# Delta rule and maxout FFN on one core: inverse squares of the key norms from one root, first diagonal blocks copied from PSUM, first solution turned in halves, weight conversions behind x

## The chip, the cores and the metric

The kernel runs on one core of a Trainium2 chip. The metric is the device time of one execution in microseconds (us), as the median of three runs. Engines are named as in the profile: PE is TensorE, DVE is VectorE, ACT is ScalarE, POOL is GpSimd, SP is SyncE, which here only issues transfers.

## The reference

Two parts follow each other. The first is a delta rule over 768 tokens for 4 batches and 8 heads of 48 dimensions; the second is a maxout FFN over 3072 tokens, with three weights 384 to 768 and one 768 to 384. All arrays are fp32.

```python
# q, k, v: [4, 8, 768, 48]   beta: [4, 8, 768]
k_n = k / (np.linalg.norm(k, axis=-1, keepdims=True) + 1e-06)
state = np.zeros((B, H, D, D), dtype=np.float32)
for t in range(S):
    kt, vt, bt = (k_n[:, :, t], v[:, :, t], beta[:, :, t, None])
    y[:, :, t] = np.einsum('bhd,bhde->bhe', q[:, :, t], state)
    v_old = np.einsum('bhde,bhd->bhe', state, kt)
    state = state + bt[:, :, :, None] * np.einsum('bhd,bhe->bhde', kt, vt - v_old)
x = y.transpose(0, 2, 1, 3).reshape(4 * 768, 384)
h = np.maximum(np.maximum(x @ w1, x @ w2), x @ w3)
out = h @ w_out
```

## The kernel before

**Tiling.** The 768 tokens of a sequence are cut into 12 chunks of 64, taken for 2 batches at a time on the 128 partitions. Two chunks for all four batches make a group of 512 rows of x, so there are 6 groups, m = 0 to 5. A chunk's recurrence needs the inverse of a triangular 64x64 matrix for each head and batch. It is made from two 32x32 diagonal blocks, inverted on DVE, and an off-diagonal part made by matmuls on PE.

**The solver.** `solve(m)` inverts the diagonal blocks of group m. It first takes the diagonal of the blocks, which holds the squared norms of the keys (`ksum`), and makes two things of it in `bl` (128x32): the norm plus 1e-6, and beta divided by its square. The root is taken on ACT (L261), and a refinement of it and all that follows on DVE (L262 to L266, then L519 to L525). `norms_of(m, bl)` turns the norms on DVE into the layout of the values (four transpositions, L281, into `nrm`); `scale` multiplies the values by them on POOL (L287). The blocks are multiplied by the factors (L538), and then come the steps, each of them one product (L552) and one difference (L556) on DVE with few columns at first. The generator yields after each step; `some(solving, n)` issues n of them between other work.

**The order of work.** There is no scheduler. Each engine executes what the Python code issued, in that order, and waits on semaphores for what it needs. `ffn(m)` is a generator over the FFN of group m; at each of its yields `i` a table (`LINKS`, `FIRST` for group 0, `EARLY_LINKS`) says which pieces of the recurrence of the next group are issued. A table entry is a letter and a number: k is `old_k` (p_k on PE, then `v_t` minus `p_k` on DVE, L743), q `old_q`, u `new` (p_u on PE from that `v_t`, L759), y `to_y`, s `step`, x `to_x`, P a Gram matrix with its mask, M a mask alone, N `load_blocks` for the group after next. In the steady table the entries around the change are

```python
5: "g2 g3 p1", 6: "u0 N0", 7: "V1 N1", 8: "s0 y0 N2", 9: "x0", 10: "k1 q1",
11: "u1 w0", 13: "y1 x1 s1", 14: "X0 w1", 16: "P0", 17: "X1 K0 K1 K2 K3",
```

`solve(m + 2)` and its head (all up to the first yield) are issued at i = 8 behind "s0 y0 N2", and its first steps at i = 9. `load_blocks` of N0, N1 and N2 issues 16 transfers each from POOL's queue (L364), with a memset ahead of each eight. It acts only while a group m + 2 exists, so in the FFNs of groups 1 to 3; the solves of groups 3, 4 and 5 start in the FFNs of groups 1, 2 and 3.

**Weights.** The FFN's weights go through a conversion: `weights()` fetches the fp32 bits in pieces of 128 columns and splits each into two halves. ACT does three scalings (L238 to L240), DVE one shift (L250) and POOL one addition (L254). `some(conv, 1)` issues one piece; the POOL addition of a piece is issued when the next piece is.

**The opening.** Before the first FFN, `keys(n)` makes the Gram matrix p_g of a unit in PSUM, ACT or DVE copies it to `at` (L423), and `to_blocks` copies four 32x32 block groups of `at` out of SBUF (L465, L467) into a tile in `wo_sb`. `first_blocks` transposes that tile on DVE (L471). Group 0 is then solved with blocks of size 32 in rows of 16, its solution is transposed as a whole (L564), copied into `ut` by `placed` (L496), and `ut` is transposed again by `halves_t` into `t` (L633, L635). Then follow `halves_z`, `halves_u`, `turn_t1`, `join_z`, `join_u` (the off-diagonal part, p_e, p_f, p_z, p_j), `old_k`, `old_q`, `new`, `to_y`, `to_x`, and the head of `solve(1)`; then the FFN of group 0 begins with p_h (L1161) and its maximum on DVE (L1175).

Of the kernel before, what the change touches and what calls it, by code (L numbers as in the profile page):

```python
# [14 lines left out]
ALU = mybir.AluOpType  # L15

C = 64
DP = 64
BL = 32
HB = 16  # L20
# [3 lines left out]
def kernel(  # L24
# [196 lines left out]
    def weights():  # L221

        waiting = None
        for dst, _, (a, b) in pieces:
            bits = staged.popleft().rearrange("p (a b two) -> p a b two", a=a, two=2)
            low, high = bits[:, :, :, 0], bits[:, :, :, 1]
            mant = work.tile([128, 384], U32, name="mant", bufs=2)
            up = work.tile([128, 384], I32, name="up", bufs=2)  # L230
            mant_v = mant.rearrange("p (a b) -> p a b", a=a)
            up_v = up.rearrange("p (a b) -> p a b", a=a)
            halves = [
                up.bitcast(t)[:, i::2].rearrange("p (a b) -> p a b", a=a)
                for i, t in enumerate((I16, FP16))
            ]

            nc.scalar.mul(mant_v.bitcast(FP32), high.bitcast(FP32), 2.0**-112)  # L238
            nc.scalar.mul(halves[0], low, 2.0**-29)
            nc.scalar.mul(halves[1], high.bitcast(FP32), 2.0**-64)  # L240
            if waiting:
                joined(*waiting)
            waiting = dst, mant, mant_v, up_v
            yield
        joined(*waiting)
        yield

    def joined(dst, mant, mant_v, up_v):
# [9 lines left out]

    def norm(out, ksum, root, t):

        nc.scalar.sqrt(root, ksum)  # L261
        nc.vector.tensor_scalar_max(t, root, 1e-30)  # L262
        nc.vector.reciprocal(t, t)
        nc.vector.tensor_tensor(out=t, in0=t, in1=ksum, op=ALU.mult)
        nc.vector.tensor_tensor(out=t, in0=t, in1=root, op=ALU.add)
        nc.vector.tensor_scalar(  # L266
            out=out, in0=t, scalar1=0.5, scalar2=1e-6, op0=ALU.mult, op1=ALU.add
        )

    def small(name, *shape):  # L270
# [27 lines left out]
    nrm_0 = const.tile([128, 2, 2, H], FP32, name="nrm_0")  # L298
    bl_0 = []

    def first_norms():
        nc.vector.transpose(out=nrm_0.rearrange("p c g h -> p (c g h)"), in_=bl_0[0])

# [150 lines left out]

    def to_blocks(n, engines):


        cc, g = divmod(n, 2)
        for i, engine in enumerate(engines):
            bb, half = divmod(i, 2)  # L460
            r, x0 = block(bb, half), 16 * cc + 8 * g
            to = in_rows(in_wo(0))[r, x0 : x0 + H]
            of = ats[n][r, :, BL * half : BL * (half + 1)]
            if engine is nc.scalar:
                engine.copy(to, of)  # L465
            else:
                engine.tensor_copy(to, of)  # L467

# [19 lines left out]

    def placed(cc, i, copy=nc.vector.tensor_copy, xs_of=slice(0, 2 * H)):
        bb, half = divmod(i, 2)  # L490
        r = block(bb, half)
        to = ut[cc][r, :, :, BL * half : BL * (half + 1)].rearrange(
            "p g h i -> p (g h) i"
        )
        of = in_rows(xs[0])[r, :, 16 * cc : 16 * (cc + 1)].rearrange("p i x -> p x i")
        copy(to[:, xs_of], of[:, xs_of])  # L496

    def solve(m):
# [11 lines left out]
        elif m > 2:  # L510
            nc.scalar.copy(y, zero.to_broadcast(y.shape))
        bl = small("bl", BL)
        norm(bl, diagonal(x), small("root_bl", BL), small("nt_bl", BL))
        if m == 1:
            y = ps_two("y_p").rearrange("p b (j i) -> p (b j) i", i=BL)
            nc.scalar.copy(y, zero.to_broadcast(y.shape))
        if m:
            norms_of(m, bl)
            nc.vector.reciprocal(bl, bl)  # L519
        else:  # L520
            bl_0.append(bl)
            bl = small("inv_bl", BL)
            nc.vector.reciprocal(bl, bl_0[0])
        nc.vector.tensor_tensor(out=bl, in0=bl, in1=bl, op=ALU.mult)
        nc.vector.tensor_tensor(out=bl, in0=bl, in1=beta_bl[:, m] if m else beta_0, op=ALU.mult)  # L525
        if m > 2:
# [8 lines left out]
        else:  # L535
            size, xv, yv = BL, x[:, None], y[:, None]
            xb, by = x, bl[:, None, :].to_broadcast([128, BL, BL])
        nc.vector.tensor_tensor(out=xb, in0=xb, in1=by, op=ALU.mult)  # L538
        yield
        for j in range(size - 1):  # L540
            a, b = j + 1, size - 1 - j
            n = BL // size
# [19 lines left out]
        if m == 0:  # L562
            back = in_rows(xs[0])
            nc.vector.transpose(out=back, in_=y.rearrange("p c i -> p i c"))  # L564
            yield
            for i in range(4):
                if i % 2:
                    n = H * (i == 3)
                    if n:
                        placed(0, i, nc.vector.tensor_copy, slice(0, n))  # L570
                    placed(0, i, nc.scalar.copy, slice(n, 2 * H))
                else:
                    placed(0, i, nc.vector.tensor_copy)
            return
# [51 lines left out]

    def halves_t(c, parts=(0, 1)):
        if c not in fine:
            fine[c] = [square("t") for g in range(2)]
        src = [ut[c % NU][:, g].rearrange("p h x -> p (h x)") for g in range(2)]  # L630
        dst = [t.rearrange("p h x -> p (h x)") for t in fine[c]]
        if 0 in parts:
            nc.vector.transpose(out=dst[0], in_=src[0])  # L633
        for bb in range(2) if 1 in parts else ():
            nc.vector.transpose(out=dst[1][rows(1 - bb)], in_=src[1][rows(bb)])  # L635

# [27 lines left out]
    def halves_z(c):  # L664
        if c > 1:
            halves_t(c)
        at = [ats[2 * c + g] for g in range(2)]
        second = ut[c % NU].rearrange("p g h (f two x) -> p g h f two x", two=2, x=HB)
        for hs, p_v, copy in heads_of(c, "p_e", BL):
            for i, h in enumerate(hs):  # L670
                for bb, g in TILES:
# [3 lines left out]
                    )  # L675
            copy(zs[c % NU][:, :, span(hs)], p_v)

# [16 lines left out]
    def join_z(c):  # L694
        at = [ats.pop(2 * c + g) for g in range(2)]
        z, second = zs[c % NU], ut[c % NU][:, :, :, BL:C]
        for hs, p_v, _ in heads_of(c, "p_z", BL):
            for i, h in enumerate(hs):
                for bb, g in TILES:
                    r = block(bb, 1)  # L700
                    nc.tensor.matmul(
                        p_v[block(bb ^ g), g, i], at[g][r, h, 0:BL], second[r, g, h]
                    )
            for bb in range(2):
                nc.scalar.copy(z[block(bb), :, span(hs)], p_v[block(bb)])

# [100 lines left out]
    def to_x(c):  # L807
# [8 lines left out]
        for g in range(2):  # L816
# [9 lines left out]
            if not c:  # L826
                nc.scalar.copy(xt[:, g], of[:, g])  # L827
        if c:
# [415 lines left out]
    load_v(0)  # L1244
    fetch(nc.sync)
    busy(6, ident)
    turn(0, (0,))
    turn(1, (0,), nc.vector.tensor_copy)
    A, V, P = nc.scalar, nc.vector, nc.gpsimd
    keys(0, None)  # L1250
    to_blocks(0, (P, P, P, P))
    turn(2, (0,))
    keys(1, None, nc.vector.tensor_copy)
    to_blocks(1, (V, V, V, P))
    turn(3, (0,))
    keys(2, None)
    to_blocks(2, (A, P, A, P))
    keys(3, None, nc.vector.tensor_copy)
    to_blocks(3, (V, A, V, P))
    first_blocks()  # L1260
    load_q(2, (nc.gpsimd, nc.gpsimd))
    turn(4, (0,))
    turn(5, (0,))
    some(solving, 1)
    keys(4)
# [3 lines left out]
    load_q(3, (nc.gpsimd, nc.gpsimd))  # L1269
    load_beta()  # L1270
    keys(6)
    gram(0, (1,), None, later=True)
    turn(7, (0,))
    turn(1, (1,))
    keys(7)
    turn(2, (1,))
    gram(1, (1,), None, later=True)
    turn(3, (1,))
    some(conv, 1)
    gram(2, (1,), None, later=True)  # L1280
    gram(3, (1,), None, later=True)
    some(solving, HB + 1)
    halves_t(0)
    halves_z(0)
    first_norms()
    some(conv, 1)
    placed(1, 0)
    scale(0, nrm_0[:, 0])
    placed(1, 1, nc.gpsimd.tensor_copy)
    blocks(1, nc.gpsimd)  # L1290
    for _ in range(2):
        fetch(nc.gpsimd)
    halves_u(0)
    turn_t1(0)
    join_z(0)
    masked(pts[0], by_par(pts[0]))
    placed(1, 2)
    join_u(0)
    masked(pts[1], by_par(pts[1]))
    old_k(0)  # L1300
    old_q(0)
    new(0)
    some(conv, 1)
    fetch(nc.gpsimd)
    load_v(1, nc.gpsimd)
    placed(1, 3)
    to_y(0)
    halves_t(1)
    solving = solve(1)
    some(solving, 1)  # L1310
    to_x(0)
    some(conv, 1)
# [18 lines left out]
        0: "e1 s0 S1 S1", 1: "f1 k1 S1 S1 S1", 2: "z1 d1 M2 S1 S1",  # L1331
        3: "j1 S1 q1 M3 S1 S1", 4: "u1 T4", 5: "y1", 6: "s1 T5", 7: "x1 T6",
        8: "T7", 14: "P4", 15: "P5", 21: "P6", 22: "P7",
# [37 lines left out]

    CONVERTED = {*range(6), *range(11, 25)}
    FETCHED = {8: 1, 12: 1, 13: 1, 14: 1, 18: 2, 19: 2, 20: 1, 21: 1}
# [100 lines left out]
```

## Time and profile before

| what | value |
|---|---|
| three runs | 512.97, 513.03, 517.85 us; median 513.03 |
| span of the profiled execution | 510.5 us |
| PE busy | 491.1 us (96%) |
| DVE busy | 349.9 us (69%) |
| POOL busy (without the issuing of transfers) | 192.7 us (38%) |
| ACT busy | 168.7 us (33%) |
| first p_h (L1161) starts | 44.39 us |
| p_u (L759) of the two stretches where group 3 and group 4 begin to be solved | 215.74 and 288.56 us |

The span is from the first to the last instruction of the profiled execution; its own time is the span and some 2.5 us around it, which gives the median of the runs. In a timeline a row says start, duration, engine, line, operation, tiles written and read, shape and count. What stands in brackets at its end is the idle time before it and what ended that. Issues of transfers stand as DMA_DIRECT2D rows on the engine whose queue issues them. Their time is the engine's even though the page does not count it as busy.

### The profile page before, as it was taken

The numbers are of one execution on the slowest core, as the hardware profiler recorded it, in microseconds if no ns is written. First come the engines' busy times: TensorE is split into PE (matmuls) and PEld (weight loads), VectorE is DVE, ScalarE is ACT, GpSimd is POOL, SyncE is SP. The second block draws the span as 40 slices with busy tenths as digits, with TensorE's granted clock in tenths as the row PEclk, the third lists the DMA queues.
The fourth block names the chain that finished last, engine by engine and source line by source line (L and its number), as shares of the span: only waits on it lengthen the run. The fifth ranks groups of instructions, "written<-read, shape, count | busy, mean of one in ns | idle before, by whom it ended". The sixth has DMA issues, their size and how long they took to land.

```text
span 510.5 us, 18528 instructions
## 1 busy us (share of the span) xinstructions
PE 491.1 (96%) x8016; PEld 333.1 (65%) x8016; DVE 349.9 (69%) x801; ACT 168.7 (33%) x320; POOL 192.7 (38%) x317
## 2 busy tenths in 40 slices
PE   7778989999999999999999999999999999999996
PEld 6567778756565565665555565555655556998796
DVE  5897799969996430899563987635897455456752
ACT  5585664884422242210252101252101412113210
POOL 7434372783491926670575770503130000000000
PEclk9755999999999999999999999999999999999999
DMA  8938869764055925353675454923343202230001
GB/s 111 192 64 221 194 151 155 195 199 100 5 148 140 175 46 130 99 143 83 144 136 130 120 137 94 174 37 92 80 116 81 44 3 64 54 71 2 0 17 46
DMA packets 106304, 53.49 MB, mean 105 GB/s; under 512 B 89712, under 2 KB 99984, under 8 KB 106224
## 3 DMA queue, kind: packets, MB, share of 16 engines
q1 hardware_dynamic: 94352, 31.35, 30.4%
q0 software_dynamic: 9472, 20.37, 16.4%
q8 instruction: 63, 1.03, 0.9%
q10 hardware_dynamic: 2400, 0.59, 0.6%
q14 instruction: 17, 0.14, 0.1%
HBM read 39.17 MB, written 13.11 MB: 102 GB/s over the span
## 4 chain that ended last, share of the span: by engine, by line
PE 73%; DVE 14%; DMA 5%; ACT 4%; SPq 2%; issue 2%; POOL 0%; DVEq 0%; ACTq 0%; POOLq 0%
PE p_h L1161 26%; PE p_o L1199 13%; PE p_o L960 9%; PE p_e L1102 3%; DVE tmp L552 3%; PE p_g L406 3%; PE p_c L1102 2%; PE p_m L894 2%; PE p_u L759 2%; DMA kmore<-in_k_dram 2%; PE p_k L731 2%; PE p_y L801 2%; DVE y_bl L556 2%; PE p_s L782 2%; PE p_j L714 1%
## 5 line engine op out<-in xcount | busy, mean ns | idle before, releaser
L1161 PE MATMUL p_h<-xt,w_sb 128*128 128x512 f32 (+1 forms) x450 | 187.5, 558 | 0.7 <-ACT xt L827 0.6
L1161 PEld LDWEIGHTS p_h<-xt,w_sb 128*128 128x128 f32 x450 | 82.3, 193 | 68.7 <-issue 61.8
L1199 PE MATMUL p_o<-wo_sb,h 128*128 128x384 f32 x192 | 65.3, 490 | 0.0
L1175 DVE TENSOR_TENSOR h<-h,p_h 128x512 f32<-128x512 f32 (+1 forms) x42 | 25.4, 606 | 53.9 <-PE p_h L1161 52.8
L552 DVE TENSOR_TENSOR tmp<-x_bl,y_bl 128x31 f32<-128x31 f32 (+20 forms) x139 | 51.3, 369 | 4.1
L556 DVE TENSOR_TENSOR y_bl<-y_bl,tmp 128x31 f32<-128x31 f32 (+20 forms) x139 | 48.5, 349 | 4.8
L1199 PEld LDWEIGHTS p_o<-wo_sb,h 128*128 128x128 f32 x192 | 35.7, 190 | 23.2
L364 POOL DMA_DIRECT2D turned<-in_q_dram x72 | 39.1, 551 | 4.3 <-POOL turned L359 2.9
L1205 ACT COPY o_sb<-p_o 128x384 f32<-128x384 f32 x16 | 7.7, 479 | 85.8 <-PE p_o L1199 79.8
L1171 ACT ACTIVATE h<-p_h 128x512 f32<-128x512 f32 x24 | 14.3, 597 | 63.4 <-PE p_h L1161 60.5
L254 POOL TENSOR_TENSOR w_sb<-mant,up 128x384 int32<-128x384 int32 x18 | 19.1, 1059 | 39.3 <-DVE mant L250 39.2
L406 PEld LDWEIGHTS p_g<-kqt 48*64 48x64 f32 x1216 | 24.6, 142 | 9.0 <-issue 6.4
L406 PE MATMUL p_g<-kqt 48*64 48x64 f32 (+1 forms) x1216 | 27.8, 242 | 0.9 <-ACT kqt L335 0.8
L789 DVE TENSOR_TENSOR st<-st,p_s 48x768 f32<-48x768 f32 (+1 forms) x18 | 17.1, 949 | 15.4 <-PE p_s L782 15.2
L120 POOL DMA_DIRECT2D kpad<-in_k_dram x32 | 21.8, 690 | 14.1 <-issue 12.7
L1199 PE MATMUL p_o<-w_sb,xt 128*128 128x384 f32 x72 | 25.2, 486 | 0.0
L139 POOL DMA_DIRECT2D v_t<-in_v_dram x14 | 11.5, 829 | 35.5 <-PE p_u L759 35.5
L390 DVE TENSOR_TENSOR pt<-p_g,mask 128x512 f32<-128x512 f32 x20 | 13.8, 688 | 15.9 <-PE p_g L406 15.8
L287 POOL TENSOR_TENSOR v_t<-v_t,nrm 128x768 f32<-128x768 f32 x12 | 17.9, 1493 | 9.0 <-DVE nrm L281 8.9
L359 POOL MEMSET turned<- 128x96 f32 x18 | 3.3, 192 | 47.6 <-DVE kqt L380 47.6
L759 PEld LDWEIGHTS p_u<-v_t,ut 64*64 64x64 f32 x768 | 13.4, 141 | 10.1 <-issue 7.8
L1199 PEld LDWEIGHTS p_o<-w_sb,xt 128*128 128x128 f32 x72 | 13.7, 190 | 9.5
(212 smaller groups left out, 837.0 us busy)
## 6 DMA issues: line engine op xcount, KB each, us to landing
out_dram<-o_sb SPq DMA_DIRECT2D x40, 96.0 KB
w_bits<-in_moe_w_dram SPq DMA_DIRECT2D x9, 384.0 KB
w_bits<-in_moe_w_dram POOLq DMA_DIRECT2D x9, 384.0 KB, 5.2
turned<-in_q_dram POOLq DMA_DIRECT2D x72, 48.0 KB, 2.9
kpad<-in_k_dram POOLq DMA_DIRECT2D x32, 96.0 KB, 6.1
y_x<-y SPq DMA_DIRECT2D x16, 192.0 KB
qall<-y_x SPq DMA_DIRECT2D x32, 96.0 KB
v_t<-in_v_dram POOLq DMA_DIRECT2D x14, 192.0 KB, 5.0
```

The costliest lines, as they stand in the source:

```text
L120: queues[bb].dma_start(out=dst[rows(bb ^ g), :, 0:D], in_=src[2 * bb + g, :, c * C : (c + 1) * C, :].rearrange("h p d -> p h d"),)
L254: nc.gpsimd.tensor_tensor(out=dst.bitcast(I32), in0=mant_v.bitcast(I32), in1=up_v, op=ALU.add)
L364: (queue, nc.gpsimd)[i].dma_start(out=t[p0 : p0 + 32, bb, at : at + NP * 2 * D].rearrange("p (j x) -> p j x", j=NP), in_=(k, q)[i][2 * bb ...
L406: nc.tensor.matmul(p_g[rows(bb ^ (g * i)), par, c0 : c0 + C * (1 + whole)], kq[:, 0], kq if whole else kq[:, i],)
L552: nc.vector.tensor_tensor(out=t_v, in0=row.to_broadcast(t_v.shape), in1=column.to_broadcast(t_v.shape), op=ALU.mult,)
L556: nc.vector.tensor_tensor(out=rest, in0=rest, in1=t_v, op=ALU.subtract)
L759: nc.tensor.matmul(p_v[rows(bb ^ g), g, i], ut[c % NU][rows(bb), g, h], rhs[rows(bb), g, h],)
L960: nc.tensor.matmul(to[:, g], a[j][:, 128 * g : 128 * (g + 1)], b[j], start=(start and g == j == 0), stop=(stop and g == 1 and j == PAIRS - 1),
L1102: nc.tensor.matmul(to, w[stays], moves, start=(n == 0), stop=(n == len(terms) - 1))
L1161: nc.tensor.matmul(p_h, w_sb[i][:, t, f * 128 : (f + 1) * 128], xt[:, t, lo : lo + w], start=(t == 0), stop=(t == KT - 1),)
L1175: nc.vector.tensor_tensor(out=h, in0=h, in1=p_h, op=ALU.max)
L1199: nc.tensor.matmul(p_o, stays, moves, start=(n == 0), stop=(n == len(terms) - 1))
```

## The change

The squared norm's inverse is now made directly: ACT takes a root of it scaled by 4e-12, DVE adds that and 1e-12 to the squared norm (this is the square of norm plus 1e-6) and takes the reciprocal. The norm itself, which only the values need, is made from this by a root on ACT and four small operations on POOL (`norms`), issued at the end of the solver's head. `norms_of`, the four transpositions on DVE, is issued at the solver's second step (j = 1) for m of 1 and up. For m = 0 the norms are turned by matmuls on PE.

```diff
-        bl = small("bl", BL)
-        norm(bl, diagonal(x), small("root_bl", BL), small("nt_bl", BL))
+        bl = small("inv_bl", BL)
+        square_bl, norm_bl = small("square_bl", BL), small("bl", BL)
+        inverse_squares(bl, square_bl, diagonal(x))
...
-        if m:
-            norms_of(m, bl)
-            nc.vector.reciprocal(bl, bl)
-        else:
-            bl_0.append(bl)
-            bl = small("inv_bl", BL)
-            nc.vector.reciprocal(bl, bl_0[0])
-        nc.vector.tensor_tensor(out=bl, in0=bl, in1=bl, op=ALU.mult)
-        nc.vector.tensor_tensor(out=bl, in0=bl, in1=beta_bl[:, m] if m else beta_0, op=ALU.mult)
+        inverse, bl = bl, small("nt_bl", BL)
+        nc.vector.tensor_tensor(
+            out=bl, in0=inverse, in1=beta_bl[:, m] if m else beta_0, op=ALU.mult
+        )
...
         nc.vector.tensor_tensor(out=xb, in0=xb, in1=by, op=ALU.mult)
+        norms(norm_bl, square_bl, inverse, small("root_bl", BL))
+        bl_of[m] = norm_bl
         yield
         for j in range(size - 1):
+            if m and j == 1:
+                norms_of(m, norm_bl)
```

with the new functions

```diff
+    def inverse_squares(out, square_of, ksum):
+        nc.scalar.activation(
+            out=square_of, in_=ksum, func=mybir.ActivationFunctionType.Sqrt,
+            scale=4.0 * EPS * EPS,
+        )
+        nc.vector.scalar_tensor_tensor(
+            out=square_of, in0=square_of, scalar=EPS * EPS, in1=ksum,
+            op0=ALU.add, op1=ALU.add,
+        )
+        nc.vector.reciprocal(out, square_of)
+    def norms(out, square_of, inverse, t):
+        mult = nc.gpsimd.tensor_tensor
+        nc.scalar.sqrt(out, square_of)
+        mult(out=t, in0=out, in1=out, op=ALU.mult)
+        mult(out=t, in0=t, in1=inverse, op=ALU.mult)
+        nc.gpsimd.tensor_scalar(
+            out=t, in0=t, scalar1=-0.5, scalar2=1.5, op0=ALU.mult, op1=ALU.add
+        )
+        mult(out=out, in0=out, in1=t, op=ALU.mult)
```

In the opening, `first_keys` takes the place of `keys` and `to_blocks`: the block groups are copied from p_g in PSUM, most of them by DVE, and ACT copies the whole of p_g to `at` (for units 2 and 3 behind the transposition's issue). The solution y is transposed in halves (`turn_back`, `turn_half`) and copied out in the order in which p_e, p_f and the rest use it; `t` is zeroed by POOL earlier and then filled by copies of 16 columns (`halves_t`). The values are scaled during the solve. The second half of x is copied by DVE. The transposition `turn(3, (1,))` moves behind `to_x`.

```diff
-    keys(2, None)
-    to_blocks(2, (A, P, A, P))
-    keys(3, None, nc.vector.tensor_copy)
-    to_blocks(3, (V, A, V, P))
+    later = [first_keys(2, (A, V, A, V)), first_keys(3, (V, A, V, V))]
     first_blocks()
+    for whole in later:
+        whole(nc.scalar.copy)
...
-    some(solving, HB + 1)
-    halves_t(0)
+    some(solving, HB)
+    turn_back(1)
+    for i in range(4):
+        placed(0, i, A.copy if i % 2 else V.tensor_copy, high)
+    turn_half()
+    halves_t(0, (V, V, P, P, V, P, V, A))
     halves_z(0)
...
+    turn_back(0)
+    for i in (1, 3, 0, 2):
+        placed(0, i, V.tensor_copy if i % 2 else P.tensor_copy, low)
     halves_u(0)
```

The weights' third fetch on SP moves behind the transfers `at_d` of the opening. Of four conversions before the FFN three are left, of which the last is behind `to_x`, and `CONVERTED` has one more place in FFN 0. In `FIRST` the mask M3, which read `pt` in SBUF, becomes P3: the Gram matrix of unit 3 by PE, masked from PSUM.

## The prediction

> **What bounds the kernel now.** I read the page first: busy times, then the slices.
>
> ```profile
> PE 491.1 (96%) x8016; PEld 333.1 (65%) x8016; DVE 349.9 (69%) x801; ACT 168.7 (33%) x320; POOL 192.7 (38%) x317
> ...
> PE   7778989999999999999999999999999999999996
> ...
> POOL 7434372783491926670575770503130000000000
> PEclk9755999999999999999999999999999999999999
> ```
>
> PE is the bound from slice 6 on. Only the first 60 us have gaps and a low clock. So a shorter opening gains what is left when PE becomes gap-free, and anything that makes PE wait later costs its full length: there is no idle time to absorb it. POOL's row has dips, but transfers that POOL issues don't count as busy. That is why I went on to the timelines of the stretches in which solve(3) and solve(4) begin, the places where the norms are moved to POOL. POOL's:
>
> ```profile
> 195.02 1.65 POOL L139 DMA_DIRECT2D v_t<-in_v_dram  x2 [13.76 <-PE p_u L759]
> ...
> 206.79 0.55 POOL L364 DMA_DIRECT2D kmore<-in_k_dram  x1 [0.29 <-POOL kmore L359]
> 209.12 3.79 POOL L364 DMA_DIRECT2D kmore<-in_k_dram  x7 [1.77 <-issue]
> 212.90 0.20 POOL L359 MEMSET kmore<- 128x96 f32 x1
> 213.39 0.55 POOL L364 DMA_DIRECT2D kmore<-in_q_dram  x1 [0.29 <-POOL kmore L359]
> 215.69 3.81 POOL L364 DMA_DIRECT2D kmore<-in_q_dram  x7 [1.75 <-DMA kmore<-in_k_dram]
> 219.50 1.49 POOL L287 TENSOR_TENSOR v_t<-v_t,nrm 128x768 f32<-128x768 f32 x1
> ...
> 291.72 4.34 POOL L364 DMA_DIRECT2D kmore<-in_q_dram  x8 [0.29 <-POOL kmore L359]
> 296.07 1.49 POOL L287 TENSOR_TENSOR v_t<-v_t,nrm 128x768 f32<-128x768 f32 x1
> ```
>
> From 195 to 219.5 POOL issues 32 transfers of the units N1 and N2 without a pause of its own, at some 0.55 us each and with short waits. The scaling of the values, next in its queue, starts when they are through, at 219.50 and, one group later, at 296.07. DVE and PE in the same two stretches:
>
> ```profile
> 207.68 0.17 DVE L262 TENSOR_SCALAR nt_bl<-root_bl 128x32 f32<-128x32 f32 x1
> 208.97 0.88 DVE L281 STREAM_TRANSPOSE nrm<-bl 64x32 f32<-64x32 f32 x4
> 213.86 0.94 DVE L743 TENSOR_TENSOR v_t<-v_t,p_k 128x768 f32<-128x768 f32 x1
> ...
> 212.97 2.84 PE L1161 MATMUL p_h<-xt,w_sb 128*128 128x512 f32 x6
> 215.74 1.38 PE L759 MATMUL p_u<-v_t,ut 64*64 64x48 f32 x64
> ...
> 288.56 1.15 PE L759 MATMUL p_u<-v_t,ut 64*64 64x48 f32 x64
> ```
>
> Norms, transpositions, early steps and L743 stand on DVE in this order; p_u needs L743's result.
>
> **The steady part: norms behind POOL's issues.** The head of the solver loses four operations on DVE, but the norm that L281 transposes now comes from four POOL operations. They stand in POOL's queue where L287 stands now: behind all the issues of N0 to N2. The four transpositions are issued at j = 1, ahead of L743. Without a wait DVE would be there early: from 207.68, an addition (0.22, as L264), reciprocal 0.35, product 0.19, L538 1.23, one maximum L1175 0.68 and the first step 0.4, 3.1 with gaps: 210.8. POOL reaches the norms only at 219.50. DVE stands still meanwhile, and behind the transpositions wait two steps, L743 and the next maximum of h; PE, at p_u, waits for L743.
>
> A POOL operation on 128x32 isn't in the trace as a product. From below: a memset of 128x96, 0.20; from above: a copy of 128x32 (L529), 0.69, once 1.23 beside a busy DVE. The products of 768 columns (1.49) and 384 columns (0.99) lie on a line that gives 0.5 at 32. DVE stands still here, so I take 0.5, four make 2.0 (0.8 to 2.8). Then DVE: transpositions 0.91 with a gap (208.97 to 209.88), step j = 1 0.51, step j = 2 0.45, L743 0.94, together 2.8.
>
> - Group 3: 219.50 + 2.0 + 2.8 = 224.3 instead of 215.74: PE stands 8.5 us.
> - Group 4: 296.07 + 4.8 = 300.9 instead of 288.56: 12.3 us.
> - Group 5 has no units N; POOL is free from 345.96 and L287 waits for the norms (it starts at 354.89 after 8.93 idle). Nothing.
> - Group 2 begins in FFN 0, where POOL's queue holds conversions, not these issues. The path there has POOL's copy of the diagonal (118.44, 1.23) and now 2.0 of norms, less 1.4 off DVE's chain; PE has a gap of 1.00 before its p_u at 130.25. Zero, within 1 us both ways.
>
> The sum is +20.8 (18.4 to 22.4). POOL's issues start from a p_u of the group before (195.02), so they shift along with PE and catch up nothing.
>
> **The clock after the stalls.** A PE that stands still that long comes back at half speed. In before this is seen after the gap from about 14.2 to 16.14:
>
> ```profile
> 12.00:14.00 2.00, 1.57 (x68) 1.46 (x68) 1.86 (x2) 0.86 (x2) 1.96 (x3) 1.00 0.82 143
> 14.00:16.00 2.00, 0.20 (x2) 0.00 (x0) 1.50 (x7) 1.71 (x4) 0.28 (x1) 0.87 1.25 193
> 16.00:18.00 2.00, 1.86 (x36) 1.56 (x40) 1.55 (x6) 0.59 (x1) 1.08 (x2) 0.50 0.87 117
> ...
> 52.00:54.00 2.00, 2.00 (x45) 1.48 (x47) 1.36 (x6) 0.00 (x0) 1.26 (x2) 0.74 0.79 223
> ```
>
> (Columns: length, then busy time and count of PE, weight loads, DVE, ACT, POOL; granted clock; DMA share; GB/s.) The clock falls to 0.50 and is back only at about 22.3, 6.2 us later; in the gap-free work from 44.39 it comes back at about 53.0, after 8.6. At half speed such a stretch loses half its length. I take the smaller, 3.1 per stall, 6.2 in all (0 to 8.6).
>
> The Trainium skill (TensorE: Matmul & The Clock Gate, Part 1, What's actually happening) has the clock halved after one idle window of about 3.4 us and full again after one busy window. By that page a stall would cost an estimated 1.7, up to 3.4 when windows lie badly, so 3.4 to 6.8 in all in place of my 6.2. The trace agrees that idle time lowers the clock, but not on the way back, which took 6.2 and 8.6.
>
> **The opening.** Copies from PSUM: DVE now makes ten at 0.42 (as L716), 4.2, in place of 0.69 + 1.11 + 0.69 + 0.70 = 3.2; +1.0 before the transposition at 12.20 (0 to +2.2, if three engines take turns at one PSUM tile). Norm chain: 14.18 to 16.81 is 2.6; root 0.26, addition 0.22, reciprocal 0.35, product 0.19 and gaps make 1.2; -1.4. But the product with beta waited 0.21 until 16.59, for a transfer by the trace; if that is beta landing, the solve begins no earlier than now. I take 0 for its start (-1.4 to +1.0).
>
> After the last step: a half transposition (0.71, as L633) in place of 1.98 stands before the first copies, -1.3; DVE's second transposition into t (0.71 + 1.44) becomes 0.71 and copies shared with POOL, which idles there (zeroing t costs it two pairs of memsets in its idle time from 21 to 33; without that cover 2 us). The copy of the second half of x moves off ACT (0.48, in series with the first), and four transpositions of turn(3,(1,)) (1.06) leave the path ahead of x. Together some -2 at the first p_h (44.39).
>
> Most is given back. The conversion of the fourth weight piece now stands where the fifth stood: POOL's addition that ends at 59.69. Less a lead of 1.3 to 2.0, it ends at 57.7 to 58.4, and the fourth p_h, now at 57.58, waits for it. From 59 to 74 DVE is the bound (steps with 0.4 us each and next to no gaps) and a mask of 0.69 becomes a Gram matrix on PE plus a mask that waits for PE. I keep -0.5 of the -2; from -3.2 (all kept, and the clock back some 2.4 us earlier) to +2.5 (front +1.0, and 1.5 for a clock that returns 3 us later). The third weight fetch moved on SP is read by ACT only after 39; it took 3.2 us from its old issue; nothing, or as long as it is late, 1 at most.
>
> **Sum.** The profiled span is 510.5, 2.5 around it give 513.0, the median. 513.0 - 0.5 + 20.8 + 6.2 = 539.5.
>
> **Rivals.**
>
> - Stalls without loss of clock: PE resumes full or nearly so. Every long gap in the opening speaks against it; that the page's rule is shorter than my rows, for a smaller loss. 513.0 - 0.5 + 20.8 = 533.3.
> - POOL comes in time, the other side. p_u isn't late if the norms are done by 215.74 - 2.8 = 212.9, so POOL must reach them by 210.9: 8.6 us earlier than L287 now, and 12.3 in group 4. It would need the transfers' issues not to hold the operations behind them. For it: issues don't count as busy. Against it: L287, ready since the transpositions at 209.85, starts at 219.50, just where the last issue ends. Only the opening would remain: 512.5, down to 509.8.
> - Only the stall of group 4 remains, POOL being early enough in group 3 because its waits for slots (1.77, 1.75) and what precedes move: 513.0 - 0.5 + 12.3 + 3.1 = 527.9. The waits are too small for 8.5.
>
> **Chances.** Main case 0.62, with its spread 530 to 547; no loss of clock 0.25; only one stall 0.05; POOL in time 0.05; worse than 547 0.03. The range 527 to 547 takes in the second case and most of the third. A measurement of this kernel tells about 1% (5.1 us) from no change. Faster by over 1% needs POOL in time and nearly the best opening: 0.02; within 1%: 0.04; slower 0.94.
>
> **What would show it.** In the new profile: DVE idle by some 10 and 14 us before the transpositions of nrm, released by POOL; PE idle by 8.5 and 12.3 before two p_u, the clock at 0.5 behind each; POOL's norms straight behind the issues into kmore; no such gap in group 5; the first p_h near 42.4 and the solve's first step near 17.6. If DVE's wait at nrm is under 3 us in groups 3 and 4, the forecast is wrong.

## The result, and the profile after

The changed kernel took 538.72 us (median of four runs, 537.22 to 540.14) against 513.49 for the kernel before in the same comparison: a ratio of 1.0473, 95% interval 1.042 to 1.0526. Every ratio is to runs of the kernel before in the same comparison (medians 513.49 to 514.81 us), without the few executions, of either kernel, that fell into a slower state. The profiled execution of the changed kernel has a span of 535.3 us, 24.8 more than the 510.5 of before. Its page:

```profile
PE 493.5 (92%) x8024; PEld 335.5 (63%) x8024; DVE 343.3 (64%) x778; ACT 168.9 (32%) x327; POOL 204.3 (38%) x349
...
PE   6878799999999999399999379999999999999996
...
POOL 6639274873747547620658732141430000000000
PEclk9667899999999999799999869999999999999999
```

PE's work is the same (493.5 us busy, 491.1 before), but its row has two holes, in slices 17 and 23, and the clock's row dips there. The timelines of these two places say why. POOL's, with what ends its stay at the transfers, in group 3 and in group 4:

```profile
215.87 3.27 POOL L386 DMA_DIRECT2D kmore<-in_q_dram  x6
219.15 0.25 POOL L281 TENSOR_TENSOR root_bl<-bl 128x32 f32<-128x32 f32 x1
...
220.12 0.25 POOL L286 TENSOR_TENSOR bl<-bl,root_bl 128x32 f32<-128x32 f32 x1
220.91 1.48 POOL L305 TENSOR_TENSOR v_t<-v_t,nrm 128x768 f32<-128x768 f32 x1 [0.54 <-DVE nrm L299]
...
302.19 4.36 POOL L386 DMA_DIRECT2D kmore<-in_q_dram  x8 [0.29 <-POOL kmore L381]
306.56 0.25 POOL L281 TENSOR_TENSOR root_bl<-bl 128x32 f32<-128x32 f32 x1
```

The first of the four norm operations starts within 0.02 us of the end of the last issue into kmore. DVE's timeline (the bracket is the idle time before the row, and what ended it):

```profile
210.22 0.19 DVE L605 TENSOR_TENSOR y_bl<-y_bl,tmp 128x31 f32<-128x31 f32 x1
220.41 0.88 DVE L299 STREAM_TRANSPOSE nrm<-bl 64x32 f32<-64x32 f32 x4 [9.99 <-POOL bl L286]
221.32 1.14 DVE L601 TENSOR_TENSOR tmp<-x_bl,y_bl 128x60 f32<-128x60 f32 x1
...
223.20 0.95 DVE L796 TENSOR_TENSOR v_t<-v_t,p_k 128x768 f32<-128x768 f32 x1
...
307.81 0.88 DVE L299 STREAM_TRANSPOSE nrm<-bl 64x32 f32<-64x32 f32 x4 [14.30 <-POOL bl L286]
```

and PE's:

```profile
212.69 2.84 PE L1214 MATMUL p_h<-xt,w_sb 128*128 128x512 f32 x6
224.24 1.96 PE L812 MATMUL p_u<-v_t,ut 64*64 64x48 f32 x64 [8.71 <-issue]
...
295.78 2.84 PE L1214 MATMUL p_h<-xt,w_sb 128*128 128x512 f32 x6
311.65 2.07 PE L812 MATMUL p_u<-v_t,ut 64*64 64x48 f32 x64 [13.03 <-issue]
```

PE's wait is put down to "issue", but the row that ends just before each p_u is DVE's L796, and that stands behind the transpositions. The table of 2-us windows (length, busy time and count of PE, weight loads, DVE, ACT, POOL, then the granted clock) shows what the waits do to the clock:

```profile
222.00:224.00 2.00, 0.00 (x0) 0.00 (x0) 1.90 (x5) 0.00 (x0) 2.00 (x4) 0.50 0.13 32
...
226.00:228.00 2.00, 2.00 (x12) 1.17 (x8) 1.90 (x6) 0.80 (x1) 0.00 (x0) 0.56 0.15 38
228.00:230.00 2.00, 2.00 (x8) 1.21 (x7) 1.83 (x6) 0.00 (x0) 0.00 (x0) 1.00 0.00 0
...
314.00:316.00 2.00, 2.00 (x4) 1.09 (x4) 1.83 (x7) 0.56 (x1) 0.00 (x0) 0.50 0.00 0
316.00:318.00 2.00, 2.00 (x6) 1.10 (x6) 1.83 (x6) 0.00 (x0) 0.00 (x0) 0.87 0.00 0
```

The starts of the 450 p_h matmuls, taken one by one in both traces, show where the 24.8 us arise. The shift against before (later is positive, places by the time in before) is:

| place in before | shift | what lies between |
|---|---|---|
| first p_h, 44.39 | +0.80 | opening up to x |
| 55.41 | -1.64 | clock back near 47, before near 53; a wait of 0.71 for a conversion |
| 62.26 | +1.38 | PE waits of 1.03 and 2.26 |
| 120.53 | +0.95 | 0.4 given back |
| 157.95 to 197.27 | -0.27 | a wait of 1.00 ahead of p_u at 130.25 is gone |
| p_u at 215.74 | +8.50 | first stall, 8.77 |
| 242.38 | +9.86 | half clock, 1.4 |
| p_u at 288.56 | +23.09 | second stall, 13.1 |
| 314.98 | +25.39 | half clock, 2.3 |
| 415.55 | +24.77 | 0.6 given back |

### The profile page after: what moved, and what is told of

Its sections match the earlier page's. It is cut to its first block, busy times and chain, and to the rows that moved or that the text cites. A ratio compares the mean times of both kernels' runs of the same rounds, so it can differ in the third digit from the quotient of the medians.

```text
span 535.3 us, 18561 instructions
## 1 busy us (share of the span) xinstructions
PE 493.5 (92%) x8024; PEld 335.5 (63%) x8024; DVE 343.3 (64%) x778; ACT 168.9 (32%) x327; POOL 204.3 (38%) x349
## 3 DMA queue, kind: packets, MB, share of 16 engines
q8 instruction: 63, 1.03, 0.8%
## 4 chain that ended last, share of the span: by engine, by line
PE 80%; POOL 6%; DVE 5%; issue 4%; DMA 3%; ACT 1%; SPq 0%; POOLq 0%; DVEq 0%
PE p_h L1214 29%; PE p_o L1252 17%; PE p_o L1013 8%; PE p_g L428 4%; PE p_u L812 3%; PE p_e L1155 3%; POOL turned L386 3%; PE p_c L1155 2%; PE p_y L854 2%; POOL kmore L386 2%; PE p_k L784 2%; PE p_j L767 2%; PE p_q L784 2%; PE p_z L756 2%; PE p_s L835 1%
## 5 line engine op out<-in xcount | busy, mean ns | idle before, releaser
L1252 PE MATMUL p_o<-wo_sb,h 128*128 128x384 f32 x192 | 67.5, 503 | 0.0
L601 DVE TENSOR_TENSOR tmp<-x_bl,y_bl 128x31 f32<-128x31 f32 (+20 forms) x139 | 52.6, 378 | 4.1
L1252 PEld LDWEIGHTS p_o<-wo_sb,h 128*128 128x128 f32 x192 | 36.8, 196 | 24.3 <-issue 1.8
L812 PE MATMUL p_u<-v_t,ut 64*64 64x48 f32 x768 | 17.0, 245 | 22.1 <-issue 22.1
L1224 ACT ACTIVATE h<-p_h 128x512 f32<-128x512 f32 x24 | 14.3, 597 | 69.1 <-PE p_h L1214 66.3
L812 PEld LDWEIGHTS p_u<-v_t,ut 64*64 64x64 f32 x768 | 15.5, 161 | 29.8 <-issue 29.0
L428 PEld LDWEIGHTS p_g<-kqt 48*64 48x64 f32 x1088 | 22.4, 141 | 9.0 <-issue 5.5
L428 PE MATMUL p_g<-kqt 48*64 48x64 f32 (+1 forms) x1088 | 25.1, 242 | 1.6 <-ACT kqt L357 1.6
L817 ACT COPY u<-p_u 128x768 f32<-128x768 f32 (+1 forms) x12 | 9.3, 772 | 41.3 <-PE p_u L812 41.3
```

Source lines behind the costliest of these rows:

```text
L428: nc.tensor.matmul(p_g[rows(bb ^ (g * i)), par, c0 : c0 + C * (1 + whole)], kq[:, 0], kq if whole else kq[:, i],)
L601: nc.vector.tensor_tensor(out=t_v, in0=row.to_broadcast(t_v.shape), in1=column.to_broadcast(t_v.shape), op=ALU.mult,)
L812: nc.tensor.matmul(p_v[rows(bb ^ g), g, i], ut[c % NU][rows(bb), g, h], rhs[rows(bb), g, h],)
L1252: nc.tensor.matmul(p_o, stays, moves, start=(n == 0), stop=(n == len(terms) - 1))
```

## The experiments

The first theory is the prediction's: DVE's four transpositions wait for norms that stand behind POOL's issues, and p_u waits behind DVE. The rivals are that the transpositions or the POOL operations cost this themselves, or that the opening takes part. Two words ahead. The description above lets the units N act in the FFNs of groups 1 to 3; the entry is evaluated for the next group, so they act in those of groups 1 and 2, where the two stalls are. And the same opening and first FFN take different times from one execution to the next: at 178 us in before's count the profiled executions of the changed kernel, e1, e4, e5 and e6, which are alike up to there, stand at -0.3, +5.5, +2.8, +2.6 and -0.9 us. So stalls are compared by what the shift gains across them, and small differences by medians.

**e1, N2 behind the norms.**

```diff
-            links(m + 1, (LAST_LINKS if m == GROUPS - 2 else LINKS).get(i, ""))
+            names = (LAST_LINKS if m == GROUPS - 2 else LINKS).get(i, "")
+            links(m + 1, names.replace(" N2", ""))
             if i > 7:
                 some(solving, 3 if i > 8 else 1)
+            if i == 8:
+                links(m + 1, "N2")
```

> The changed kernel with one move: the 16 transfers of unit N2 are issued behind the head of the solver, so POOL's four norm operations come ahead of them. Theory (the norms are late because they stand behind N2's issues in POOL's queue): DVE's wait ahead of the four transpositions falls from 10.0 and 14.3 us to under 1 and about 2, the idle PE time before the two p_u from 8.7 and 13.0 to under 1, the clock stays at 1.0 there, and the time is about 513 (538.7 less 21.7 of idle time less 3.2 of clock). Rival (transpositions at j = 1, or the four POOL operations themselves, hold DVE): the two gaps stay above 5 us each and the time above 527.

Measured: 514.51 us, ratio to before 1.0004 (0.9972 to 1.0036). PE and DVE in e1's timeline:

```profile
218.50 2.84 PE L1214 MATMUL p_h<-xt,w_sb 128*128 128x512 f32 x6
221.27 1.15 PE L812 MATMUL p_u<-v_t,ut 64*64 64x48 f32 x64
...
216.43 0.88 DVE L299 STREAM_TRANSPOSE nrm<-bl 64x32 f32<-64x32 f32 x4 [0.22 <-POOL bl L286]
```

p_u follows p_h at once, and DVE waits 0.22 us in group 3 and 1.56 in group 4, in place of 10.0 and 14.3. The same operations at the same places cost nothing when 16 issues stand behind them and not ahead. The whole loss is gone.

**e2, the opening of before with the norms as in e1.** The kernel before, with the inverse squares, the POOL norms and the late transpositions for groups 3 to 5, and e1's move of N2:

```diff
-        bl = small("bl", BL)
-        norm(bl, diagonal(x), small("root_bl", BL), small("nt_bl", BL))
+        if m > 2:
+            bl, square_bl, norm_bl = small("inv_bl", BL), small("square_bl", BL), small("bl", BL)
+            inverse_squares(bl, square_bl, diagonal(x))
+        else:
+            bl = small("bl", BL)
+            norm(bl, diagonal(x), small("root_bl", BL), small("nt_bl", BL))
...
+            if m > 2 and j == 1:
+                norms_of(m, norm_bl)
```

> The kernel before with its own opening and its norms for groups 0 to 2; groups 3 to 5 take the inverse squares and the POOL norms of the change, and N2 is issued behind them as in e1. With e1 it differs by the opening alone. Theory (the opening is worth what the shift of p_h shows at 160 us, -0.3 us): 513.5, that is e1 within 0.5 us. Rival (the opening brings the 2 us by which the solution is ready sooner): e1 is faster than this one by 2 or more.

Measured: 513.39 us, ratio 1.0006 (0.998 to 1.0033), the same as e1. The changed opening is worth nothing that these runs can tell from zero; the two intervals leave room for some 2 us either way.

**e3, before with the norm part alone.** As e2, but with N2 left ahead of the head of the solver.

> The kernel before with the norm part of the change alone, for groups 3 to 5: roots and inverse squares as changed, four POOL operations, transpositions at j = 1; N2 stays ahead of them, the opening is that of before. Theory (the loss comes from POOL's queue alone): 513.5 + 8.7 + 13.0 + 3.2 = 538.4, within 1.5 us of the changed kernel. Rival (the opening or its other clock history takes part in the loss): 530 or less.

Measured: 540.84 us (two runs), ratio 1.052 (1.0468 to 1.0572). Its table of waits (us in total, times, longest) has DVE's and PE's:

```profile
DVE nrm L306 <- POOL bl L293: 24.3, 3, 13.7
...
PE p_u L796 <- issue: 21.8, 3, 12.4
```

The norm part alone makes the loss, and more than expected by 2 us; its profiled execution was already 3.4 us behind at 178 us, ahead of the first stall, so nothing is read from the difference. Across the two stalls and the half clock behind them its shift gains 25.4 us (3.38 to 28.82), in the changed kernel 25.7 (-0.27 to 25.39).

**e4, matmuls in the stalls.** To take the clock's share by itself:

```diff
         for hs, p_v, copy in heads_of(c, "p_u", D):
+            for _ in range({5: 10, 7: 16}.get(c, 0)):
+                nc.tensor.matmul(
+                    p_v[:, 0], ident, w_sb[1][:, 0, 0:DM].rearrange("p (h x) -> p h x", x=D)
+                )
```

> The changed kernel with matmuls added on PE in front of the two late p_u (10 for the first, 16 for the second, 128x384, some 0.69 us each, into the area of p_u, overwritten by it): PE is busy for about 6.9 and 11 us of the two waits, and nothing else changes. Theory (3.2 us of the loss is the clock that fell during the waits): the clock stays at 1.0 behind both, the two p_u start where they did (shift from before 8.5 and 21 instead of 8.5 and 23), and the time is about 535.5. Rival (the rest beyond the two waits comes from DVE's backlog behind them): the time stays at 538.7.

Measured: 537.93 us, ratio 1.0466 (1.0432 to 1.05). e4's timeline of PE at the first stall:

```profile
218.59 6.61 PE L811 MATMUL p_u<-w_sb,ident 128*128 128x384 f32 x20
227.44 1.34 PE L816 MATMUL p_u<-v_t,ut 64*64 64x48 f32 x64 [2.23 <-issue]
```

and its windows behind the first and the second (columns as above):

```profile
228.00:230.00 2.00, 2.00 (x57) 1.52 (x50) 1.90 (x6) 0.80 (x1) 0.28 (x1) 1.00 0.48 124
...
316.00:318.00 2.00, 2.00 (x5) 1.09 (x4) 1.83 (x6) 0.00 (x0) 0.00 (x0) 0.50 0.01 1
```

Behind the first stall the clock stays at 1.0, and the shift doesn't grow after p_u (11.70 at p_u, 11.65 at the next p_h; the changed kernel: 8.50 and 9.86). Behind the second the clock still fell, for 3.41 us by the trace's clock record, and the shift grows by 1.8 (2.3 in the changed kernel): 2.45 us without a matmul were left there. So the clock's share at the first stall is 1.4 us and it is the clock. The expected total was missed: the median fell by 0.8, not 3.2, of which the second stall and, in the profiled execution, a start 3.1 us slower by 178 us explain most.

**e5, half of N2's issues on SP.**

```diff
-                load_blocks(4 * (m + 2) + i)
+                load_blocks(4 * (m + 2) + i, nc.sync if i == 2 else nc.gpsimd)
```

> The changed kernel, with the eight key transfers of unit N2 issued from SP's queue in place of POOL's; the eight query transfers stay on POOL ahead of the norms. A dose: in the changed kernel's trace the key issues hold POOL for 6.1 us in group 3 (206.55 to 212.67) and 6.8 in group 4 (294.94 to 301.69). Theory: the idle PE time before the two p_u falls by just these, from 8.7 and 13.0 to some 2.6 and 6.3, the norms come straight behind the query issues, and the time is about 524 to 526 (the clock still falls in group 4). Rival (POOL is held by the landing of transfers or by slots, whoever issues them): the gaps fall by under 3 us each and the time stays above 532.

Measured: 525.52 us (two runs), ratio 1.022 (1.017 to 1.027). PE in e5's timeline:

```profile
220.86 1.15 PE L812 MATMUL p_u<-v_t,ut 64*64 64x48 f32 x64 [2.48 <-issue]
...
299.43 2.07 PE L812 MATMUL p_u<-v_t,ut 64*64 64x48 f32 x64 [5.83 <-issue]
```

Eight issues less ahead of the norms take 6.2 and 7.2 us off the stalls; 2.6 and 6.3 were expected to be left. It is POOL's time at the issues, not the landing: the same bytes still move.

**e6, transpositions at step 16.**

```diff
-            if m and j == 1:
+            if m and j == (16 if m > 2 else 1):
```

> The changed kernel with the four transpositions of the norms issued at the solver's step 16 in place of step 1 for groups 3 to 5; POOL's queue as changed. Theory (what costs is the place of DVE's wait, ahead of the L796 that p_u needs): DVE's wait falls to under 1 us, p_u waits for nothing, about 513 to 515; POOL's scaling waits for DVE instead, by up to 5 us, in idle time. Rival (late norms hold the group's work in any place): over 525.

Measured: 517.68 us, ratio 1.007 (1.0035 to 1.0104). Of its timeline, one row of POOL and one of PE:

```profile
231.25 1.47 POOL L305 TENSOR_TENSOR v_t<-v_t,nrm 128x768 f32<-128x768 f32 x1 [10.82 <-DVE nrm L299]
...
389.90 2.81 PE L1214 MATMUL p_h<-xt,w_sb 128*128 128x512 f32 x6 [1.51 <-DVE xt L914]
```

Both stalls are gone, so what costs is a wait on DVE ahead of L796, not late norms as such. But it isn't free: 513 to 515 was expected. POOL's scaling waits 10.82 us in place of at most 5, the kpad issues behind it are late, and the shift grows by 3.2 between 258 and 402 us. PE's waits there, where the kernel before has none, are that of 1.51 for DVE's copy of x, 1.1 in all at p_z for a transfer of the solution, and 0.3 with no releaser; which late issue lies behind each is open.

**e7, two waits of the opening taken off** (on e1):

```diff
-        nc.scalar.copy(nrm_0.rearrange("p c g h -> p (c g h)"), p_n)
+        return lambda: nc.scalar.copy(nrm_0.rearrange("p c g h -> p (c g h)"), p_n)
...
-    scale(0, nrm_0[:, 0])
     some(solving, HB)
...
         placed(0, i, A.copy if i % 2 else V.tensor_copy, high)
+    norms_turned()
+    scale(0, nrm_0[:, 0])
...
-    halves_t(1, (V, V, P, P, V, V, P, P))
     to_x(0)
+    halves_t(1, (V, V, P, P, V, V, P, P))
```

> e1 with two orders of its opening changed. The root's copy out of PSUM and the scaling of the first values come behind the first copies of the solution (in the changed kernel the scaling ran on POOL beside the step at 25.85 us, which took 1.46 in place of 0.21), and the copies of halves_t(1) come behind x (they stood ahead of the copy of x on DVE, 43.06 to 44.5). Theory: the step takes 0.2 again, the first p_h starts 1.2 to 2.4 us sooner than in the changed kernel, and some 1 to 2 of it is kept: 511.5 to 513. Rival (PE's instructions are not loaded in time in the stretch from 56 to 62, so that what is ready sooner waits there): the first p_h comes sooner, but behind the gaps before p_z and p_q nothing is left: as e1, 513 to 514.5.

Measured: 514.59 us, ratio 0.9995 (0.9967 to 1.0024). Nothing came of it, and not by the rival's reason alone. The last step takes 0.21 again, but the four copies of L685, now beside the scaling, take 2.66 in place of 1.37. From the transposition of the blocks to the first p_h it is 31.5 us, in the changed kernel 31.6. The scaling only met another DVE operation.

**e8, block copies out of SBUF** (on e7; the lines of the opening are those of before):

```diff
-    first_keys(0, (V, V, P, P), nc.scalar.copy)
+    keys(0, None)
+    to_blocks(0, (P, P, P, P))
...
-    later = [first_keys(2, (A, V, A, V)), first_keys(3, (V, A, V, V))]
+    keys(2, None)
+    to_blocks(2, (A, P, A, P))
+    keys(3, None, nc.vector.tensor_copy)
+    to_blocks(3, (V, A, V, P))
```

> e7 with the block copies of before: ACT or DVE copies the whole of p_g to at, and the four block groups are copied from there out of SBUF. Theory (block copies from PSUM cost 1.4 us, as the transposition moved from 12.20 to 13.60): the transposition starts at about 12.2 and the first step of the solver 1.2 to 1.4 sooner than in e7, unless beta is late; the first p_h as much sooner, the time by up to 1 less than e7. Rival (beta lands at about 16.5, or the work behind sets the end): the first step at 17.5 as in e7, and the same time.

Measured: 513.42 us, ratio 0.9978 (0.995 to 1.0007). The first step starts at 16.55, in the changed kernel at 17.58, and the product with beta ran at 15.50 without a wait: beta isn't late. The last of the four Gram matrices starts at 9.88 in the kernel before and in the changed one, and at 10.25 in e8; the transposition starts at 12.20, 13.60 and 12.58. So the copies from PSUM cost 1.4, as expected; 0.4 of it doesn't show in the first step because e8's keys came later. In e8's timeline of PE:

```profile
42.91 1.53 PE L1228 MATMUL p_h<-xt,w_sb 128*128 128x256 f32 x6 [0.30 <-ACT mant L237]
...
61.46 1.62 PE L798 MATMUL p_q<-st,kqt 48*64 48x48 f32 x50 [2.70 <-issue]
```

The first p_h is 1.48 us ahead of before, the second 4.11. Then PE waits 0.91, 1.18 and 2.70 in the middle of p_f, p_z and p_q and 1.07 for a conversion, the clock is at half from 60.75 to 67.58, and at 66.84 the shift is +1.89. All is given back.

**e9, fewer small matmuls in that stretch** (on e8):

```diff
-        3: "j1 S1 q1 P3 S1 S1", 4: "u1 T4", 5: "y1", 6: "s1 T5", 7: "x1 T6",
+        3: "j1 S1 S1 S1", 4: "u1 P3 T4", 5: "q1 y1", 6: "s1 T5", 7: "x1 T6",
```

> e8 with two entries of FIRST moved: P3 from FFN position 3 to 4 behind u1, q1 from 3 to 5 ahead of y1. In e8's trace PE stands 2.70 us in the middle of p_q with no releaser, 1.50 after a 16 KB instruction packet has landed (58.45 + 1.51), and the first p_h, 1.5 us sooner than before, has turned into 1.9 later at 66. Theory (PE's instructions come no faster than a 16 KB packet in some 5 us there, and two small groups between two p_h need more): with 192 matmuls' and loads' worth of instructions behind one and two p_h more, the gap is spread: no wait over 1.5 us, the shift against the kernel before at 72 us between 0 and 1 in place of 1.9, the time 0.5 to 2 less than e8's 513.4. Rival (p_q waits for its own operand): the gap goes along with p_q to its new place, 2 us or more, and the time stays.

Measured: 512.85 us, ratio 0.9979 (0.9952 to 1.0005). e9's p_q:

```profile
67.89 1.15 PE L798 MATMUL p_q<-st,kqt 48*64 48x48 f32 x64
```

It no longer waits, so the wait wasn't p_q's own. The longest wait of this kind left is 1.00 at p_z, and the shift at 72.37 is +1.32, with a stretch of half clock in it, against the 0 to 1 expected. e8 and e9 are each some 25 us faster than the changed kernel; against the kernel before, neither interval excludes no change.

## Why the prediction was right, step by step

**The stalls (20.8, measured 21.9).** Place, cause and length held, and e1, e3 and e5 show the cause: put the issues behind the norms and it goes, put the norms alone into the old kernel and it comes, halve N2's issues and it shrinks by their time. Two terms inside were off and nearly cancelled. The four POOL operations took 1.2 us with their gaps (219.15 to 220.37), not 2.0: the line through 768 and 384 columns lies too high at 32. DVE's part up to p_u took 3.8, not 2.8, for L601 on 128x60 took 1.14 beside the start of POOL's scaling, 0.22 elsewhere; my sum had DVE alone there. In group 4 the issues ended 0.5 later than before, with PE's shift taken off. That POOL catches nothing up was right: v_t's load still starts from the p_u of the group before.

**The clock (6.2, measured 3.7).** The mechanism was right and the size was not. I had taken 3.1 per stall from the opening, where PE comes back with gaps; here it is busy at once, and half speed lasts 3.5 us of busy time behind the first stall and about 5 behind the second (windows above), 1.4 and 2.3 of loss. My estimate from the Trainium skill (TensorE: Matmul & The Clock Gate, Part 1, What's actually happening), 3.4 to 6.8 in all, holds it at its low end. The trace's clock record has the two stretches at half clock 6.83 and 13.65 us long, two and four times 3.41; a good part of each lies in the wait itself, where it costs nothing.

**The opening (-0.5, measured +0.95 up to 120 us).** Wrong in its parts. At the first p_h I had -2 and measured +0.80. The rows of the changed kernel that show it:

```profile
13.60 1.95 DVE L511 STREAM_TRANSPOSE x_bl<-wo_sb 128x1024 f32<-128x1024 f32 x1
...
25.85 1.46 DVE L601 TENSOR_TENSOR tmp<-x_bl,y_bl 128x30 f32<-128x30 f32 x1
...
44.48 0.56 DVE L880 COPY xt<-p_x 128x384 f32<-128x384 f32 x1
...
45.19 2.36 PE L1214 MATMUL p_h<-xt,w_sb 128*128 128x256 f32 x6 [0.29 <-DVE xt L880]
```

The transposition started 1.4 later (I had 1.0) and the norm chain gave that back, so the solve's start was even, as taken, but by luck: I had taken it from beta landing, and e8's beta wasn't late. What I missed is that POOL's scaling, moved into the solve, stands beside a DVE step, which took 1.46 in place of 0.21, and that DVE's copy of x stands behind four copies for t (from 43.06), so the copy that left ACT met a queue on DVE. In these rows that is some 1.7 of the 2.8 us (1.25 at the step, 0.4 at the copy); the rest isn't traced, and e7, which took both off, gained nothing up to the first p_h. The next part I had only as the low end: the clock came back 6 us sooner. At 62.26 us that was lost to waits I had not thought of:

```profile
PE p_q L784 <- issue: 2.3, 1, 2.3
PE p_z L756 <- issue: 1.0, 1, 1.0
...
PE p_h L1214 <- POOL w_sb L258: 0.7, 1, 0.7
```

(the table of PE's waits between 40 and 75 us). The third row is the conversion's wait at a p_h, 0.7, inside the 0.1 to 0.8 I had, though at the third and not at the fourth.

**Group 2 (0, measured -1.2)** lay a little outside the 1 us that I gave it; the wait of 1.00 ahead of its p_u is gone.

**The rivals.** Without the loss of clock it would have been 533.3; the clock fell, and e4 shows its share at the first stall. Both stalls came, so "only the stall of group 4" is out. "POOL in time" was the one that e1 then built: what it needed, the norms ahead of N2's issues, gives e1's 514.51, no change that can be told from zero.

**The total.** 539.5 against 538.72 is closer than its parts. The terms add up to 26.5 us and the traces have 24.8; the clock was 2.5 too high, the stalls 1.1 too low and the opening 1.5 too low at 120 us, of which group 2 took 1.2 back. That these errors differ in sign is luck; that the two stalls make the bulk is not.

## What to carry to other kernels

An operation moved to an engine that looks idle goes behind all that stands in that engine's queue, and issues of transfers, which count as no busy time, can hold it for 10 us or more. Before moving work, read the target queue's rows at that very place, and what stands behind the waiter on its own engine; the order of two statements (e1) was worth some 24 us here, the moved work itself nothing that could be measured. In an opening, a gain at one point is only kept if the next limits, here operations on DVE beside POOL's and the loading of PE's instructions, leave it.

## What the hardware showed that I had not expected

PE waits that no semaphore ends come 1.3 to 1.7 us behind a 16 KB instruction packet. In the trace's packets of the instruction queue one lands at 60.90 and p_q goes on at 62.21, one at 55.01 and p_z at 56.67 (changed kernel); 59.96 and 61.46 (e8); 64.54 and 65.93 (p_u, before). From one packet to the next are 5 to 6 us there, while groups of 64 small matmuls with their weight loads take 1.1 us each. e9, with fewer of them there, removes the longest wait. The Trainium skill (Runtime: NRT & Kernel Launch, Instruction fetch mechanics) has 256 instructions in such a block and the cost of crossing from one to the next mostly hidden. In this stretch PE waits 1.3 us in the kernel before and 4.8 in e8. No run changed the loading itself, but the traces leave little else. Count the instructions of PE's queue in each of the eleven traces: the waits over 0.4 us with no releaser, other than those ahead of the two late p_u, number 18, and all stand at instruction 1985, 2241, 2497, 2753, 3009 or 7105, within one. These lie whole multiples of 256 apart, whether p_f, p_z, p_j, p_q, p_u, p_s or p_h stands there, and each wait ends 1.3 to 1.7 us behind a packet's landing.

DVE and POOL hold each other up: with POOL's scaling beside them, a DVE step of 0.21 took 1.46, one of 0.22 took 1.14, and four copies of 1.37 took 2.66. The other way round, POOL's first norm operation of group 1, at 47.84 us in the changed kernel, took 1.22 beside a DVE product (L583), and 0.25 in groups 3 and 4.
